# One x turn for four head pairs, one turn for k and q, and a new table of orders and homes

## The chip, the core and the metric

The kernel runs on one core of a Trainium2 chip. Its engines are PE (TensorE, the matrix engine), DVE (VectorE), ACT (ScalarE), POOL (GpSimd) and SP (SyncE, which here only issues transfers). Each engine works through its own list of instructions in order, and waits at an instruction until what it needs is there. The metric is the device time of one execution in microseconds (us), as the median of several runs.

## The reference

Sparse attention, and a maxout layer behind it. Of the attention there are 4 batches, 8 heads, 768 positions and 64 columns a head:

```python
k_sum = k.reshape(B, H, nb, block, D).max(axis=3)       # 24 blocks of 32 keys
v_sum = v.reshape(B, H, nb, block, D).mean(axis=3)
scores_l = scale * q @ k^T, kept where |i - j| < 16
scores_s = scale * q @ k_sum^T + log(32)
a = softmax over both together
attn = a @ concat(v, v_sum)
x = attn.transpose(0, 2, 1, 3).reshape(3072, 512)
g = maximum(x @ w1, x @ w2)                             # 512 -> 1024
out = g @ w_out                                         # 1024 -> 512, float32
```

## The kernel before

**Maxout.** The kernel uses max(h1, h2) = h1 + relu(h2 - h1). It makes wd = w2 - w1 (four tiles of 256 columns) and w1o = w1 · w_out once, and then out = x·w1o + relu(x·wd)·wo. Matmuls are in bf16. On PE, L829 is x·wd (128x256 each), L856 is x·w1o, L863 is g·wo (both up to 128x512), and L813 makes w1o.

**Attention.** Heads go in pairs (4 pairs a batch), queries in groups of 256 (3 groups a batch). For a pair k and q are loaded in float32 (`land`), cast to bf16 (`kqb`), turned so that the head's columns lie on partitions, and k is placed with its block maxima in `kx` (L565 copies, the maxima are L619). Scores (L661) of two pairs and one group fill two banks of PSUM; exp on ACT gives `pb` (L675), DVE masks it (L685), values (L717) multiply with `vx`, and DVE divides by the sum, which gives one half `xs` of the group's x (L741: 128x512, two pairs). x must be turned as well, into `xt`, ahead of L829.

**Turns.** In the first batch, and for k and q of some pairs later, PE turns (L593, L756) and an engine copies the result out of PSUM. For the other three batches x is turned by a DMA transpose that SP issues (L747, 128x4x128: four blocks of 128x128 for one half, so two transfers a group). For the head pairs of `CFG["turn"]` = 22 23 30 31 32 33 (batch, pair) k and q are turned by DMA as well (L597, 128x6x128: one transfer for k, one for q, into `kt`).

**What sets the order.** Each step is a task in one list. A list scheduler (`Plan.run`) goes through time, and gives each free engine the ready task with the lowest number in `CFG["prios"]`; `CFG["engines"]` has a letter per task, its home (P POOL, D DVE, A ACT, S SP, T PE). Tiles come from rings: a task that needs a new tile waits until one of the ring is free. So the two tables and the sizes of the rings decide the order on all five engines, and it is fixed at build time. SP issues all loads, all turns by DMA and nearly all stores, in one order: an issue stands behind those ahead of it. Besides what its data needs, each issue waits for the landing of the transfer issued eight before it.

In the program's order PE ends its turns of batch 0 and w1 first, with fillers (L303) where it would idle; then comes the first L813, once w_out is cast (`wo`, L565); from there on maxout groups and attention of later batches alternate until the last stores.

## Time and profile before

| | |
|---|---|
| median of 3 runs | 170.51 us (169.4, 170.51, 171.54) |
| profiled execution | 169.97 us |
| its span (first to last instruction) | 168.2 us, so 1.77 lies around it |
| PE busy | 159.7 us (95%) |
| DVE, ACT, POOL busy | 104.0, 104.5, 43.1 us |
| moved by DMA | 36.68 MB, mean 218 GB/s |
| turns by DMA | 18 of x, 12 of k or q |

The page's rows of tenths cut the span into 40 equal slices; a digit is the busy share of a slice (9 is 90% or more). A row of a group of instructions has line, engine, operation, out<-in with partitions x elements, count, busy us and mean ns, and the idle time of the engine just ahead of them with what ended it. The chain of waits follows back from the last instruction to whatever released it at each step: start, duration, engine or transfer. SPq is a transfer's issue on SP.

### The profile page before, as it was taken

How to read it: one execution, taken by the hardware profiler on the slowest of the kernel's cores; microseconds unless marked ns; L12 is line 12 of the kernel's file. 1: busy time of each engine (PE TensorE's matmuls, PEld its weight loads, DVE VectorE, ACT ScalarE, POOL GpSimd, SP SyncE). 2: the span in 40 equal slices, each digit the busy share in tenths (PEclk: the TensorE clock that was granted, in tenths of full speed). 3: DMA queues.
4: the chain of work that ended last, by engine and by line, in shares of the span. 5: the costliest groups of instructions: out<-in, count | busy, mean ns of one | idle time of the engine just before them, and what ended most of it. 6: DMA issues, size and time to landing. Idle time of an engine off the chain costs nothing.

```text
span 168.2 us, 4640 instructions
## 1 busy us (share of the span) xinstructions
PE 159.7 (95%) x1918; PEld 105.6 (63%) x1918; DVE 104.0 (62%) x207; ACT 104.5 (62%) x148; POOL 43.1 (26%) x73
## 2 busy tenths in 40 slices
PE   6999999989999999999999999979997999999992
PEld 4768757765676555667577555737564558568462
DVE  4778688663397898787695573849913867023031
ACT  4576888783697998887993578953365652024111
POOL 7506575056534000356330203330300000000000
PEclk9999999999999999999999999999999999999999
DMA  5999999999999999999888998989889336211033
GB/s 166 337 227 329 283 348 351 375 376 313 302 281 320 304 277 233 290 179 216 173 190 241 293 170 212 248 116 238 163 251 162 94 66 181 41 62 64 4 125 125
DMA packets 69829, 36.68 MB, mean 218 GB/s; under 512 B 54640, under 2 KB 65776, under 8 KB 69808
## 3 DMA queue, kind: packets, MB, share of 16 engines
q1 hardware_dynamic: 69664, 36.32, 86.1%
q8 instruction: 15, 0.25, 0.7%
q10 hardware_dynamic: 144, 0.07, 0.1%
q14 instruction: 6, 0.05, 0.1%
HBM read 25.17 MB, written 6.29 MB: 187 GB/s over the span
## 4 chain that ended last, share of the span: by engine, by line
PE 70%; DMA 14%; SPq 9%; POOL 3%; issue 1%; DVE 0%; ACT 0%
PE banks L863 24%; PE banks L829 20%; PE banks L856 11%; DMA land<-in_moe_w_out_dram 6%; DMA land<-in_v_dram 4%; PE banks L813 4%; SPq L463 4%; PE banks L717 4%; PE banks L661 3%; DMA kt<-kqb 3%; SPq L454 3%; PE banks L593 2%; DMA xt<-xs 1%; SPq L597 1%; PE banks L537 1%; POOL vx L565 1%
## 5 line engine op out<-in xcount | busy, mean ns | idle before, releaser
L829 PE MATMUL banks<-xt,wd 128*128 128x256 bf16 x384 | 46.2, 273 | 1.5 <-DMA xt<-xs 1.2
L863 PE MATMUL banks<-wo,g 128*128 128x512 bf16 (+2 forms) x208 | 46.8, 363 | 0.0
L829 PEld LDWEIGHTS <-wd 128*128 128x128 bf16 x384 | 37.2, 98 | 10.3 <-issue 1.5
L863 PEld LDWEIGHTS <-g 128*128 128x128 bf16 x208 | 19.0, 98 | 17.1
L675 ACT ACTIVATE pb<-banks 128x1024 bf16<-128x1024 f32 x24 | 23.8, 1021 | 8.1 <-PE banks L661 8.0
L838 ACT ACTIVATE g<-banks 128x512 bf16<-128x512 f32 x27 | 16.0, 596 | 20.1 <-PE banks L829 19.9
L856 PE MATMUL banks<-w1o,xt 128*128 128x512 bf16 (+2 forms) x104 | 24.6, 363 | 0.0
L840 DVE TENSOR_SCALAR g<-banks 128x512 bf16<-128x512 f32 x21 | 14.3, 687 | 10.1 <-PE banks L829 10.0
L619 DVE TENSOR_REDUCE ks<-kx 128x24 bf16<-128x768 bf16 x16 | 15.1, 949 | 5.7 <-ACT kx L565 5.3
L565 ACT COPY o<-banks 128x512 f32<-128x512 f32 (+1 forms) x16 | 9.1, 575 | 15.3 <-PE banks L863 13.2
L685 DVE TENSOR_TENSOR pb<-pb,mask 128x1024 bf16<-128x1024 bf16 (+1 forms) x24 | 12.6, 557 | 7.8 <-ACT pb L675 7.7
L565 ACT CAST kqb<-land 128x768 bf16<-128x768 f32 x14 | 13.9, 995 | 3.9 <-DMA land<-in_q_dram 1.9
L741 DVE TENSOR_TENSOR xs<-banks,inv 128x512 bf16<-128x512 f32 x24 | 15.9, 678 | 0.3
L565 DVE COPY o<-banks 128x512 f32<-128x512 f32 (+1 forms) x10 | 6.0, 608 | 13.9 <-PE banks L863 13.9
L856 PEld LDWEIGHTS <-xt 128*128 128x128 bf16 x104 | 9.3, 98 | 8.3 <-DMA xt<-xs 0.2
L565 POOL COPY vx<-vx 32x128 bf16<-32x128 bf16 (+5 forms) x10 | 7.6, 769 | 21.7 <-DVE vx L491 12.5
L303 PE MATMUL banks<-ident,identity 128*128 128x256 bf16 x70 | 10.9, 308 | 1.6 <-DVE identity L354 1.6
L661 PEld LDWEIGHTS <-kx 64*128 64x128 bf16 x416 | 7.0, 94 | 7.5 <-issue 7.4
L717 PEld LDWEIGHTS <-pb 128*64 128x64 bf16 (+1 forms) x384 | 8.9, 110 | 4.0 <-issue 1.9
L717 PE MATMUL banks<-vx,pb 128*64 128x65 bf16 (+1 forms) x384 | 11.0, 196 | 0.0
L593 PE MATMUL banks<-ident,kqb 128*128 128x128 f32 x60 | 10.0, 282 | 0.3 <-ACT kqb L565 0.2
L565 DVE CAST kqb<-land 128x768 bf16<-128x768 f32 x12 | 8.2, 693 | 3.3 <-DMA kt<-kqb 1.9
(84 smaller groups left out, 183.9 us busy)
## 6 DMA issues: line engine op xcount, KB each, us to landing
land<-in_k_dram SPq DMA_DIRECT2D x16, 384.0 KB, 6.2
land<-in_q_dram SPq DMA_DIRECT2D x16, 384.0 KB, 5.9
land<-in_v_dram SPq DMA_DIRECT2D x16, 384.0 KB, 6.3
out_dram<-o SPq DMA_DIRECT2D x19, 256.0 KB, 3.9
land<-in_moe_w_dram SPq DMA_DIRECT2D x8, 512.0 KB, 8.2
land<-in_moe_w_out_dram SPq DMA_DIRECT2D x4, 512.0 KB, 9.7
out_dram<-o SPq DMA_DIRECT2D x4, 224.0 KB, 4.3
xt<-xs SPq DMA_TRANSPOSE x18, 2.6
```

The costliest lines, as they stand in the source:

```text
L565: {"D": nc.vector.tensor_copy, "A": nc.scalar.copy, "P": nc.gpsimd.tensor_copy}[e](out=o, in_=i)
L593: nc.tensor.transpose(out=bank(ps)[:, 128 * j:128 * j + 128], in_=src.ap[:].bitcast(F32)[:, 128 * j:128 * j + 128], identity=ident32[:])
L619: op("D", 0.95, lambda e: nc.vector.tensor_reduce(out=ks.ap[:, 0:nb], in_=free(kt(), 128, [256, NM], [192, 2], [32, 2], [1, 32]), axis=AX. ...
L675: op("A", {"A": 1.03}, lambda e: nc.scalar.activation(out=spread(pb.ap[:, 0, 0:1], [192, 8], [128, 2], [1, 64]) if PW > 128 else spread(pb ...
L685: nc.vector.tensor_tensor(out=o, in0=o, in1=spread(mask[:, 2 * u:2 * u + 1, 0:1], [0, n], [64, 2], [1, 64]), op=ALU.mult)
L717: nc.tensor.matmul(out=o, lhsT=p[r], rhs=vx[b].ap[r, par, hp + n, 2 * grp + u, a, 0:D + 1], start=(PW == 128 or par == 0), stop=(last and ...
L741: op("D", 0.69, lambda e: nc.vector.tensor_tensor(out=x.ap[:].rearrange("p n u a d -> p n (u a) d"), in0=spread(bank_tile[:, ps.ap, 0:1], ...
L829: nc.tensor.matmul(out=bank(ps)[:, 256 * s:256 * s + 256], lhsT=wd[n].ap[:, c, 128 * s:128 * s + 128], rhs=x.ap[:, c, :], start=(c == 0), ...
L838: nc.scalar.activation(out=o, in_=bank(ps), func=ACT.Relu)
L840: nc.vector.tensor_scalar_max(out=o, in0=bank(ps), scalar1=0.0)
L856: nc.tensor.matmul(out=bank(ps, c1 - c0), lhsT=x.ap[:, c, sl], rhs=w1o[c].ap[:, cols], start=(c == 0), stop=False)
L863: nc.tensor.matmul(out=bank(ps, c1 - c0), lhsT=g.ap[:, f, sl], rhs=wo[f // 2].ap[:, f % 2, cols], start=False, stop=(f == FC - 1))
```

## The change

Three edits to tiles and transfers, and a new pair of tables.

- x of a group is written into one tile of all four head pairs (`xs`, 128x1024, a ring of three instead of four halves) and turned by one transfer of eight blocks, issued with the second half. The first batch keeps its halves turned by PE.
- k and q of a head pair turned by DMA are cast into the two halves of one tile (`kqm`, a ring of two) and turned by one transfer of twelve blocks into a double `kt` tile (a ring of four).
- To fit, the rings `kqb` (pairs turned by PE) and `o` (outputs) have three tiles instead of four.
- Both tables are replaced in full: the order of all engines changes, and the home of many casts, copies and relus.

```diff
@@ -28,40 +28,40 @@
 CFG["prios"] = list(map(int, """
-36 42 59 141 97 66 223 24 166 102 61 5 160 80 103 211 41 43 38 67 83 12 32 33 49 203 16 170 18 63 98 19 7 118 153
...
+21 237 67 7 280 2 17 63 36 37 59 48 6 33 112 10 49 238 1 23 52 15 120 114 107 9 191 53 14 16 31 102 92 61 24 367 295
...
 """.split()))
 CFG["engines"] = "".join("""
-PDDDPPADDDPPPPPPDPSSSDDDATDASSSDDPPTAASSSPPDPTAASSSPDPPTDDSSDPTASSPDTASSPATDSSDATASPSPSASPDTDTADPDADDTATADPPADATATDD
...
+DPDDPDDPDDPDPPPPPPSSSAPAATADSSSAPDPTDDSSSAAAPTDDSSSDPPDTDDSSPPTASSDPTASSDATDSSDATASASDSASPDTDTDDDDADPTATADPDPDPTPTDD
...
 """.split())
@@ -316,7 +316,8 @@
         return spread(t[:, at:at + 1], *dims)
 
     land = Ring(tiles("land", 13, [128, 1024], F32))
-    kqb = Ring(tiles("kqb", 4, [128, J * 2 * D], BF16))
+    kqb = Ring(tiles("kqb", 3, [128, J * 2 * D], BF16))
+    kqm = Ring(tiles("kqm", 2, [128, 2, J * 2 * D], BF16))
     kxr = Ring(tiles("kx", 4, [128, KW], BF16))
     qxr = Ring(tiles("qx", 6, [128, S], BF16))
     PW = 128 if CFG["cols"] else 192
@@ -325,11 +326,11 @@
     stg = Ring(tiles("sums", 2, [128, H // 2, VW], BF16))
     apart = tiles("apart", 2, [128, H, VW], BF16)
     ksr = Ring(tiles("ks", 3, [128, 32], BF16))
-    ktr = Ring(tiles("kt", 6, [128, J, 128], BF16))
-    xsr = Ring(tiles("xs", 4, [128, 2, 2, 2, D], BF16))
+    ktr = Ring(tiles("kt", 4, [128, 2, J, 128], BF16))
+    xsr = Ring(tiles("xs", 3, [128, NP, 2, 2, D], BF16))
     xtr = Ring(tiles("xt", 6, [128, KC, GT], BF16))
     gr = Ring(tiles("g", 3, [128, FC, GT], BF16))
-    osr = Ring(tiles("o", 4, [128, d_model], F32))
+    osr = Ring(tiles("o", 3, [128, d_model], F32))
     wd = [Buf(Ring([t])) for t in tiles("wd", 4, [128, KC, 256], BF16)]
     w1br = Ring(tiles("w1b", 2, [128, KC, 256], BF16))
     w1b = [Buf(w1br) for _ in range(4)]
@@ -572,15 +573,15 @@
     def prep(b, hp, prio, k_on, q_on, kp, qp, tail_on):
         kx[b, hp] = Buf(kxr)
         tag = f"{b}{hp}"
-        pss = []
+        pss, by_dma = [], f"{b}{hp}" in CFG["turn"]
+        both = Buf(kqm), Buf(ktr)
         for n, eng in enumerate((k_on, q_on)):
-            by_dma = f"{b}{hp}" in CFG["turn"]
-            f, src, ps = kqin[b, hp, n], Buf(kqb), Buf(ktr) if by_dma else Buf(banks, "kq")
+            f, src, ps = kqin[b, hp, n], both[0] if by_dma else Buf(kqb), both[1] if by_dma else Buf(banks, "kq")
             pss.append(ps)
 
             def cast(f=f, src=src, n=n):
                 if by_dma:
-                    return (src.ap[:].rearrange("p (j h d) -> p h j d", h=2, d=D),
+                    return (src.ap[:, n].rearrange("p (j h d) -> p h j d", h=2, d=D),
                             landed(f, 2, J * D).rearrange("p h (j d) -> p h j d", d=D))
                 return (src.ap[:].rearrange("p (i h d j) -> p h i j d", h=2, d=D, j=2),
                         landed(f, 2, J * D).rearrange("p h (i j d) -> p h i j d", d=D, j=2))
@@ -594,15 +595,17 @@
                                         in_=src.ap[:].bitcast(F32)[:, 128 * j:128 * j + 128], identity=ident32[:])
 
             if by_dma:
-                op("S", 0.65, lambda e, src=src, ps=ps: nc.sync.dma_start_transpose(out=ps.ap[:], in_=src.ap[:]),
-                   read=[src], write=[ps], prio=prio, issue=1.35, words=60, label=f"turn {'kq'[n]}{tag}")
+                if n:
+                    op("S", 1.3, lambda e, src=src, ps=ps: nc.sync.dma_start_transpose(
+                        out=ps.ap[:].rearrange("p n j t -> p (n j) t"), in_=src.ap[:].rearrange("p n c -> p (n c)")),
+                       read=[src], write=[ps], prio=prio, issue=1.7, words=60, label=f"turn kq{tag}")
             else:
                 op("T", J * 0.056, lambda e, turn=turn: turn(), words=J, read=[src], write=[ps], prio=prio, label=f"turn {'kq'[n]}{tag}")
 
         kps, qps = pss
 
         def order(ps, *dims):
-            return spread(ps.ap[:].rearrange("p j t -> p (j t)") if by_dma else bank(ps, S, BF16), *dims)
+            return spread(ps.ap[:, 0].rearrange("p j t -> p (j t)") if by_dma else bank(ps, S, BF16), *dims)
 
         def kt():
 
@@ -643,7 +646,7 @@
 
         def q_of(n, r, c0, c1):
             t = qx[b, hp + n].ap
-            return (t if len(t.shape) == 2 else t[:].rearrange("p j t -> p (j t)"))[r, c0:c1]
+            return (t if len(t.shape) == 2 else t[:, 1].rearrange("p j t -> p (j t)"))[r, c0:c1]
 
         def mm():
             if mask_on == "T":
@@ -731,23 +734,27 @@
             op("T", 0.26 if b else 0.51, lambda e, n=n: mm(n), words=16 if b else 32, read=[pb, ready[b, hp + n], *([] if b else [apart_of[hp + n]])],
                touch=[vx[b]], write=[ps], prio=prio, label=f"values {tag}{n}")
         inv = Buf(invr)
-        x = Buf(xsr)
+        whole = xt_on == "S"
         if hp == 0:
             xt[b, grp] = Buf(xtr)
-        x_t = xt[b, grp]
+        if hp == 0 or not whole:
+            xs[b, grp] = Buf(xsr)
+        x, x_t = xs[b, grp], xt[b, grp]
+        at_x = hp if whole else 0
         op("D", 0.21, lambda e: nc.vector.reciprocal(
             out=inv.ap[:], in_=spread(bank_tile[:, ps.ap, D:D + 1], [512, 2], [D + 1, 4])),
            read=[ps], write=[inv], prio=prio, label=f"inv {tag}")
         op("D", 0.69, lambda e: nc.vector.tensor_tensor(
-            out=x.ap[:].rearrange("p n u a d -> p n (u a) d"),
+            out=x.ap[:, at_x:at_x + 2].rearrange("p n u a d -> p n (u a) d"),
             in0=spread(bank_tile[:, ps.ap, 0:1], [512, 2], [D + 1, 4], [1, D]),
             in1=spread(inv.ap[:, 0:1, 0:1], [4, 2], [1, 4], [0, D]), op=ALU.mult),
            read=[ps, inv], write=[x], prio=prio, label=f"x {tag}")
-        if xt_on == "S":
-            op("S", 0.45, lambda e: nc.sync.dma_start_transpose(
-                out=x_t.ap[:, hp:hp + 2, :].rearrange("p h (u n) -> p (h u) n", u=2),
-                in_=x.ap[:].rearrange("p h u a d -> p (h u a d)")),
-               read=[x], write=[x_t], prio=prio, issue=1.3, words=60, label=f"xt {tag}")
+        if whole:
+            if hp:
+                op("S", 0.85, lambda e: nc.sync.dma_start_transpose(
+                    out=x_t.ap[:].rearrange("p h (u n) -> p (h u) n", u=2),
+                    in_=x.ap[:].rearrange("p h u a d -> p (h u a d)")),
+                   read=[x], write=[x_t], prio=prio, issue=1.4, words=60, label=f"xt {tag}")
             return
         xp = Buf(banks, "x")
 
```

SP's list goes from 122 to 107 rows, PE's fillers from 70 to 77; the number of other matmuls stays. Where PE goes from 64-wide attention groups to 512-wide groups there are 21 places instead of 18. Behind the edits lines move: L597 becomes L599, L747 L754, L829 L836, L856 L863, L863 L870, L565 L566, L741 L747, L874 L881.

**SP, late in batch 2: turns for batches 2 and 3 of attention.** `xt` are x turns, `kt` turns of k and q, `land` loads, `out_0` stores. Before:

```order
L747 DMA_TRANSPOSE xt0_113<-xs3_112 128x4x128
L597 DMA_TRANSPOSE kt5_108<-kqb1_76 128x6x128
L747 DMA_TRANSPOSE xt2_115<-xs0_109 128x4x128
L454 DMA land0_62<-in_q_dram 128x12x64
L597 DMA_TRANSPOSE kt0_103<-kqb3_78 128x6x128
L454 DMA land10_72<-in_q_dram 128x12x64
L597 DMA_TRANSPOSE kt1_104<-kqb2_77 128x6x128
L747 DMA_TRANSPOSE xt0_113<-xs2_111 128x4x128
L597 DMA_TRANSPOSE kt2_105<-kqb3_78 128x6x128
L597 DMA_TRANSPOSE kt3_106<-kqb1_76 128x6x128
L597 DMA_TRANSPOSE kt4_107<-kqb2_77 128x6x128
L874 DMA out_0_dram<-o2_124 128x512
```

And now, from the turn of the first of batch 3's head pairs on:

```order
L599 DMA_TRANSPOSE kt2_106<-kqm1_79 128x12x128
L754 DMA_TRANSPOSE xt0_111<-xs2_110 128x8x128
L599 DMA_TRANSPOSE kt3_107<-kqm0_78 128x12x128
L881 DMA out_0_dram<-o2_122 128x512
L881 DMA out_0_dram<-o0_120 112x512
L883 DMA out_0_dram<-o0_120 16x512
L599 DMA_TRANSPOSE kt0_104<-kqm1_79 128x12x128
L754 DMA_TRANSPOSE xt1_112<-xs0_108 128x8x128
L599 DMA_TRANSPOSE kt1_105<-kqm0_78 128x12x128
L881 DMA out_0_dram<-o1_121 128x512
L881 DMA out_0_dram<-o2_122 128x512
L881 DMA out_0_dram<-o0_120 128x512
```

The loads among the turns are gone from here (they stand further ahead), and no three turns of k and q stand in a row any more: a turn of a pair has an x turn or stores between it and the next.

**SP, the start: the last weights.** Before:

```order
L774 DMA land6_68<-in_moe_w1_dram 128x4x256
L454 DMA land7_69<-in_k_dram 128x2x384
L799 DMA land8_70<-in_moe_w_out_dram 128x2x512
L799 DMA land9_71<-in_moe_w_out_dram 128x2x512
L799 DMA land10_72<-in_moe_w_out_dram 128x2x512
L799 DMA land11_73<-in_moe_w_out_dram 128x2x512
L774 DMA land12_74<-in_moe_w2_dram 128x4x256
L454 DMA land1_63<-in_k_dram 128x2x384
```

Now:

```order
L781 DMA land6_68<-in_moe_w1_dram 128x4x256
L806 DMA land7_69<-in_moe_w_out_dram 128x2x512
L455 DMA land8_70<-in_k_dram 128x2x384
L806 DMA land9_71<-in_moe_w_out_dram 128x2x512
L806 DMA land10_72<-in_moe_w_out_dram 128x2x512
L806 DMA land11_73<-in_moe_w_out_dram 128x2x512
L455 DMA land12_74<-in_k_dram 128x2x384
L455 DMA land0_62<-in_k_dram 128x2x384
L455 DMA land1_63<-in_k_dram 128x2x384
L781 DMA land2_64<-in_moe_w2_dram 128x4x256
```

The first w_out load has changed places with a k load, and the last w2 load stands behind three k loads.

More of the change, by code (lines that the diff above doesn't have):

```diff
@@ L30 @@
 CFG["prios"] = list(map(int, """
[25 rows of a table removed]
[25 rows of a table added]
 """.split()))
 CFG["engines"] = "".join("""
[L58 to L64 removed]
+DPDDPDDPDDPDPPPPPPSSSAPAATADSSSAPDPTDDSSSAAAPTDDSSSDPPDTDDSSPPTASSDPTASSDATDSSDATASASDSASPDTDTDDDDADPTATADPDPDPTPTDD
+DPAAATDTDDPPPATATDDTDTATDDTATATDDTDTATDDTDTATDDTDTATDDTDSSSASSSPSSSDSSSADPDPPPPPTDDDDDDTATDDPDPAPTDTADDPADTADTDDTADT
+DDTADTDDDTPTADDDDDDTATADAAADTADTDDSTADTDDSTADTDDSSSSDSSSDSSSPSSSADPAADPDSTAAPADATATDDPPADATATADADDDTADTDDTADTDDTADTD
+DAASADPPPAPSADPPPTADTDDSTADTDDSTADTDDSSSSASSSASSSASSSAPDDPPDPPTAAAPAPDSADPPAADSDDDPPTADTDDTADTDDTADTDDADSADPDAPPSDDD
+PATADTDDSTADTDDSTADTDDSTTATTATTATTDTDTDTATATTTDSTTTDSTATATDTDTTTDSTTTASTATATATATTTASTTTDSTDTDTATDTTTASTTTDSTDTATATDT
+TTASTTTASTATDTDTATTTDSTTTASTATDTDTDTTTDSTTTASTATDTATATTTASTTTASTATDTDTDTTTASTTTDSTATATATATTTASTTTASTDTATDTATTTDSTTTA
+STATDTATDTTTASTTTASTTTDATTTDS
 """.split())
```

6 lines of the change are left out of this document (removed), and 48 rows, old and new, of the table turn.

## The prediction

> **What bounds the kernel now.** I read the page first, for the busiest engine, its clock and the DMA engines.
>
> ```profile
> span 168.2 us, 4640 instructions
> ...
> PE 159.7 (95%) x1918; PEld 105.6 (63%) x1918; DVE 104.0 (62%) x207; ACT 104.5 (62%) x148; POOL 43.1 (26%) x73
> ...
> PEclk9999999999999999999999999999999999999999
> DMA  5999999999999999999888998989889336211033
> ```
>
> TensorE works 95% of the span at full granted clock; the DMA engines are full for its first three quarters. Then stretches (each row: PE busy, PEld, DVE, ACT, POOL, granted clock, DMA share, GB/s).
>
> ```profile
> 37.30:165.00 127.70, 125.51 (x1382) 79.78 (x1381) 76.83 (x147) 77.47 (x108) 25.00 (x33) 1.00 0.83 194
> 0.00:37.30 37.30, 34.01 (x537) 25.81 (x537) 26.66 (x59) 26.99 (x41) 18.11 (x40) 1.00 1.04 309
> 165.00:168.20 3.20, 0.20 (x4) 0.03 (x1) 0.52 (x2) 0.00 (x0) 0.00 (x0) 1.00 0.37 123
> ```
>
> There are three stages. Up to 37.30 the program waits for bytes (DMA share 1.04). From there to 165.00 PE is busy 125.51 of 127.70 and idle 2.19. The last 3.20 are copies and stores. PE's waits name the idle time:
>
> ```profile
> PE banks L829 <- DMA xt<-xs: 1.2, 1, 1.2
> PE banks L661 <- DMA kt<-kqb: 1.0, 1, 1.0
> PE banks L813 <- POOL wo L565: 0.8, 1, 0.8
> ```
>
> The first two are the whole 2.19 of the middle stage; the third ends the start. The chain of waits (start, duration, what) shows how they came about.
>
> ```profile
> 26.75 9.40 DMA land<-in_moe_w_out_dram
> 36.21 1.05 POOL wo L565
> 37.30 2.75 PE banks L813 x12
> ...
> 105.65 0.97 PE banks L856 x4
> ...
> 108.58 2.32 SPq L597
> 111.00 2.49 DMA xt<-xs
> 113.53 1.91 PE banks L829 x16
> ...
> 118.91 0.86 PE banks L856 x4
> ...
> 124.01 5.13 DMA kt<-kqb
> 129.28 0.41 PE banks L661 x16
> ...
> 151.28 4.37 PE banks L829 x40
> ```
>
> The start ends with a w_out load landing at 36.2 and its cast. At 113.5 PE waits for an x turn that stood on SP behind a k/q turn holding SP for 2.32. At 129.3 it waits for a k/q turn that took 5.13 to land. So at most 2.19 can be had from the change in the middle stage; anything else must come from the start or the tail.
>
> **The change, part by part.** The sum runs against the profiled execution: 169.97, span 168.2 and 1.77 around it; the median of the runs is 0.54 higher.
>
> *Work on PE: +0.2 to +0.3.* Matmuls are the same in number, save seven fillers (L303) more, all in the start. The new order goes from the 64-wide attention groups to 512-wide ones 21 times instead of 18. In the chain four L856 take 0.97 where attention stands ahead of them (105.65) and 0.86 elsewhere (118.91), so three more switches cost about 0.3 at most. Middle work becomes 125.5 + 0.2 = 125.7.
>
> *The start: +0.15.* PE waits for the second w_out load to be issued (wo0). The k load and the first w_out load ahead of it have only changed places, so it lands at 36.2 again. Its cast moves from POOL to ACT.
>
> ```profile
> 36.21 1.04 POOL L565 CAST wo<-land 128x1024 bf16<-128x1024 f32 x1 [0.23 <-DMA land<-in_moe_w_out_dram]
> 38.93 1.05 ACT L565 CAST wo<-land 128x1024 bf16<-128x1024 f32 x1 [1.27 <-DMA land<-in_moe_w_out_dram]
> 40.45 2.35 POOL L777 TENSOR_TENSOR wd<-land,land 128x1024 bf16<-128x1024 f32 x1 [1.63 <-DMA land<-in_moe_w_dram]
> 31.16 1.22 DVE L777 TENSOR_TENSOR wd<-land,land 128x1024 bf16<-128x1024 f32 x1 [1.35 <-DMA land<-in_moe_w_dram]
> ```
>
> ACT's cast takes 1.05, POOL's 1.04: w1·wo starts at 37.45. The PE work ahead of it ends by 36.95 by my count, so half a microsecond covers it. The last w2 load goes behind three k loads: it landed at 40.4 (POOL's subtraction began there) and now lands near 43.6. POOL's 2.35 becomes DVE's 1.22, behind a relu already in DVE's queue: wd2 is ready at about 45.7, and PE first reads it at about 46.1. Nothing is lost, with 0.4 in hand; a load 1 us later costs 0.6.
>
> *Turns, their price.* No row has an 8- or 12-block turn. Of the present ones (issue min/median/max ns; landing us):
>
> ```profile
> L747 SPq DMA_TRANSPOSE xt<-xs x18: 1195/1216/2818, 68.5 to 142.6; - x18
> ...
> DMA to landing us min/median/max: 2.4/2.6/4.7
> ```
>
> ```profile
> L597 SPq DMA_TRANSPOSE kt<-kqb x12: 1222/1368/3827, 73.9 to 124.0; - x12
> ...
> DMA to landing us min/median/max: 2.7/2.8/4.7
> ```
>
> Four blocks of 128x128 (128 KB) hold SP 1.22, six (192 KB) 1.37: 0.075 a block, so about 1.5 for eight and 1.8 for twelve. For landing I look at two x turns nearly alone (40 slices of 0.15 us, from 140 on):
>
> ```profile
> DMA  8999998993000000499996100599960000000000
> GB/s 300 451 355 369 369 396 328 382 369 82 14 0 14 27 27 27 90 230 232 225 137 33 17 5 0 102 215 215 213 125 4 0 0 0 0 0 0 0 0 0
> ```
>
> The last hump is one turn: about 215 GB/s for 0.6 us, out of a landing of 2.6. The rest is fixed. Twice the bytes add 0.6 to an x turn (3.2) and 0.9 to a k/q turn (3.7). From below: as today, 2.6 and 2.8. From above: two of today's in series, 5.2 and 5.6. I take 3.2 and 3.7 and keep both ends.
>
> The Trainium skill, "DMA: Bandwidth & Descriptors", section "Anatomy of one DMA", fits a transfer as some 2.0 us fixed plus its bytes at 436 GB/s; by it the new turns would be estimated at 2.6 and 2.9. The trace agrees on the fixed part and not on the rate (215), so I don't use it; the sum would be the same by either.
>
> *Turns, what they are late for.* I lay PE's groups of the new order end to end from 37.45, 0.109 for each L829 (40 in 4.37) and 0.216 for a 512-wide one (4 in 0.86). Behind the first read of the last x tile (xt5 of batch 3) stand 56 of the first and 70 of the second kind: 6.1 + 15.1 = 21.2. PE ends near 164.0, so the tile is wanted at 142.8. Its last half leaves DVE at about 138.0, and its turn goes out behind xt4's, at 138.3: landed at 141.5. **Slack 1.3.** The same count for the others (wanted, landed):
>
> - batch 1 x tiles: 74.2 / 72.1, 86.0 / 82.1, 91.7 / 89.4;
> - batch 2 x tiles: 106.9 / 103.7, 110.4 / 108.3, 116.5 / 114.9;
> - batch 3 xt3 and xt4: 137.1 / 134.6, 141.9 / 140.0;
> - batch 3 keys: turns issue at about 102.9, 106.0, 109.6 and 112.6 (before, the last four stood between 115 and 125.5). The last needs two casts on POOL that start once the turn of 106.0 has landed (109.7) and given its kqm tile back; it lands at 116.3, is copied on DVE from 119.4 on (behind an o copy that waits for PE) and its kx is ready at 123.5; PE wants it at 124.5. So landing has 3.1 to spare before DVE, and DVE's chain 1.0.
>
> So both present waits, 2.19, go: the k/q turns come about 10 us earlier, and no x turn has three k/q turns ahead of it. What is late next is xt4 and xt5 of the last batch and kx's chain on DVE.
>
> *Halves that wait.* An x turn now waits for the second half; the first half gets no head start of its own. The wanted/landed list has this in it already (the second half decides). Each half is one row of 0.68:
>
> ```profile
> L741 DVE TENSOR_TENSOR xs<-banks,inv 128x512 bf16<-128x512 f32 x24 | 15.9, 678 | 0.3
> ```
>
> *Shorter rings.* Three o tiles instead of four: a copy waits for the store three tiles back, and relus and casts on DVE and ACT stand behind it.
>
> ```profile
> out_dram<-o SPq DMA_DIRECT2D x19, 256.0 KB, 3.9
> ```
>
> At 3.9 the tightest, the o2 copy on DVE at 107.9, has its store (issued near 101.9) landed at 105.8: 2.1 in hand. At the end stores meet quiet queues; two copies there stand about 1 us clear. I cost it at 0; a store slower by 3 us costs 1 each time.
>
> *Small waits.* A dozen places stand within 0.4 of late (wd2; the vx cast near 72; a mask near 82.5). From below they cost nothing; at a third of them 0.3 each is 1.2. I take 0.9.
>
> **Sum.** 37.45 + 125.7 + 0.9 + 3.2 = 167.2 of span, 1.0 below 168.2. Own time 169.0; on the median's scale **169.5**.
>
> **Rivals.**
>
> - *B, the gain is eaten.* The start slips (wd2 1 us later: +0.6) and the small waits reach 1.2: span 168.1, time 170.4. For it: the start is DMA-bound at share 1.04, and a changed load order reaches PE at once there. Against: the bytes ahead of wo0 are the same.
> - *C, slower: the turns are pulled into full DMA engines.* Of stretches of ten:
>
> ```profile
> 50.00:60.00 10.00, 10.00 (x128) 6.27 (x126) 8.07 (x17) 8.77 (x14) 2.15 (x5) 1.00 1.15 308
> 60.00:70.00 10.00, 10.00 (x152) 5.18 (x151) 8.63 (x20) 8.90 (x14) 1.64 (x2) 1.00 1.18 266
> ...
> 100.00:110.00 10.00, 10.00 (x112) 6.25 (x109) 6.01 (x11) 8.87 (x12) 2.77 (x2) 1.00 1.04 216
> ...
> 130.00:165.00 35.00, 35.00 (x360) 22.99 (x356) 13.63 (x26) 11.21 (x17) 0.00 (x0) 1.00 0.29 80
> ```
>
> All loads and all k/q turns are now to be done by 116 instead of 129, with the same bytes, while 100 to 110 is at share 1.04 already. Loads in the crowd land in about 6:
>
> ```profile
> land<-in_v_dram SPq DMA_DIRECT2D x16, 384.0 KB, 6.3
> ```
>
> Were the turns to land in 6.3, x tiles (3.1 later) would miss by 1.0, 1.0 and 1.5 in batches 1 and 2 and by 1.8 in batch 3, 1.8 in all, since a wait shifts what comes after it. The last keys would come 2 x 2.6 = 5.2 late with 4.1 to spare: 1.1, to be added if the turns themselves shift with PE. Sum +2.9: span 170.1, time 172.4. It decides from landings of about 4.5 for x (smallest slack 1.3) and of 5.7 for k/q. For it: the 5.13 in the chain. Against: the medians of 2.6 and 2.8 were taken in this same crowd. At 7.5 it would be 174 and more.
> - *D, little comes together.* The first wait goes and a like one comes, at xt4 or at kx: one of the two, +1.1, time 170.6; counted with B.
> - *E, no wait at all and a start as before.* 37.3 + 125.7 + 3.2 = 166.2, time 168.5. More would need an earlier start, and wo0's load keeps its place.
>
> **How the numbers follow.** Forecast 0.45 (168.8 to 170.2), B with D 0.22 (170.2 to 171.5), C 0.27 (171 to 175, most near 172.4), E 0.06. A change within 2% (167.1 to 173.9) is about what a measurement of this kernel can't tell from none. Faster by more needs a span under 164.8, 1.4 below E: 0.03. Slower by more is the upper third of C: 0.1. The range leaves out half of E and the upper end of C: 168.2 to 173.2.
>
> **What would show it.** The 1.2 and 1.0 of the two DMA waits gone; the w1·wo start at 37.3 to 37.6; x turns landing near 3.2 and k/q turns near 3.7; PE busy 125.6 to 125.9 from there on; idle in the middle under 1.2; the tail at 3.2. I am wrong if the turns land in over 4.5, if PE waits for kx or xt in batch 3, if a copy of o waits for its store, or if the start moves by over 0.5.

## The result, and the profile after

The changed kernel takes **170.62 us** (median of 20 runs, 169.93 to 171.97), the kernel before 169.44 (20 runs, 167.99 to 171.54): a ratio of **1.0095, 95% interval 1.007 to 1.0119**. It is slower by about 1%, where I had forecast 0.6% faster. By the bound of 2% it is no change; by its interval it is slower. Ratios below leave out executions more than 1.5% above the fastest of the same kernel; where a kernel spreads so widely that this matters, the median of all its runs stands beside the ratio.

The profiled execution of the changed kernel (169.93) is its fastest of 20, and that of the kernel before (169.97) lies above its median, so these two pages look alike though the kernels are not. I read the page first (busy time, granted clock, DMA share in tenths), and then three stretches cut at the first w1·wo matmul and at PE's end (PE, PEld, DVE, ACT, POOL busy, clock, DMA share, GB/s).

```profile
span 168.1 us, 4611 instructions
...
PE 157.8 (94%) x1903; PEld 106.4 (63%) x1925; DVE 105.6 (63%) x208; ACT 104.1 (62%) x137; POOL 48.0 (29%) x83
...
PEclk9999999999999999999999999999999999999999
DMA  5999999999999998999999999999400739000314
```

```profile
36.97:164.80 127.83, 124.39 (x1364) 79.46 (x1385) 77.37 (x145) 79.61 (x106) 28.29 (x40) 1.00 0.83 190
0.00:36.97 36.97, 33.45 (x539) 26.97 (x540) 27.87 (x62) 24.46 (x32) 19.71 (x43) 1.00 1.06 315
164.80:168.10 3.30, 0.00 (x0) 0.00 (x0) 0.33 (x2) 0.00 (x0) 0.00 (x0) 0.90 0.50 167
```

The DMA engines are now full without a break until about 118 us, and then nearly idle for ten. The middle stretch is 127.83 long; in the kernel before, from 37.30 to the end of its last matmul at 165.21, it was 127.91. (Some 21 matmuls are missing from the records of this stretch, 1364 beside 1385 weight loads, so its busy time reads too low; I go by lengths.) PE's waits:

```profile
PE banks L863 <- DMA xt<-xs: 0.8, 1, 0.8
PE banks L820 <- ACT wo L566: 0.5, 1, 0.5
PE banks L863 <- ACT o L566: 0.4, 1, 0.4
```

Both waits of the kernel before are gone: L836 waits for no x turn at 113, and L664 for no k/q turn at 129. In their place stand 0.8 for another x turn and 0.4 for an o copy. The chain of waits shows where the 0.8 is from:

```profile
26.42 9.38 DMA land<-in_moe_w_out_dram
35.88 1.05 ACT wo L566
...
104.45 5.38 DMA kt<-kqm
...
110.60 1.52 ACT kx L566
...
112.62 1.23 SPq L599
...
113.90 3.83 DMA xt<-xs
...
117.78 1.04 PE banks L863 x4
```

A k/q turn lands after 5.38; ACT and then SP stand behind it; SP issues the next k/q turn at 112.2 (the chain counts it from 112.62, when ACT is done with the copy and the relu behind it) and only then, at 113.9, the last x turn of batch 2, which lands 3.83 later. It is the same pattern as in the kernel before, one tile further on.

One profiled execution of each is too few here, so the kernels were profiled again, unaltered. "Start" is the start of the first w1·wo matmul, "middle" from there to the end of PE's last matmul, "tail" the rest of the span:

| kernel | start | middle | tail |
|---|---|---|---|
| before | 37.30, 36.51, 37.03, 36.40: mean 36.81 | 127.91, 127.93, 127.80, 128.32: mean 127.99 | 2.99, 2.96, 2.97, 2.98: mean 2.98 |
| changed | 36.97, 38.08, 37.74, 36.84, 38.77: mean 37.68 | 127.83, 128.07, 127.89, 127.84, 127.46: mean 127.82 | 3.30, 3.45, 3.37, 3.42, 3.37: mean 3.38 |
| difference | +0.87 | -0.17 | +0.40 |

The sum is +1.10, beside the 1.18 between the medians. So the middle, where the gain was to be, gave 0.17; start and tail, which I had left nearly as they were, took 1.27.

PE's waits in the middle can be added up by execution. All those of 0.15 and more make 2.19, 1.92, 1.60 and 1.81 in the kernel before (mean 1.9) and 1.21, 1.73, 1.49, 1.47 and 1.04 in the changed one (mean 1.4). So 0.5 of waits went, and PE's time without them grew by the other 0.3. The page on which the forecast rested shows the largest waits of the four: its x turn and its k/q turn, 2.19 together, make 1.54, 1.16 and 1.32 in the other three.

### The profile page after: what moved, and what is told of

It is laid out like the page before. It is cut to its first block, busy times and chain, and to the rows that moved or that the text cites. A ratio compares the mean times of both kernels' runs of the same rounds, so it can differ in the third digit from the quotient of the medians.

```text
span 168.1 us, 4611 instructions
## 1 busy us (share of the span) xinstructions
PE 157.8 (94%) x1903; PEld 106.4 (63%) x1925; DVE 105.6 (63%) x208; ACT 104.1 (62%) x137; POOL 48.0 (29%) x83
## 4 chain that ended last, share of the span: by engine, by line
PE 75%; DMA 13%; ACT 4%; issue 2%; DVE 1%; SPq 1%; POOL 1%; POOLq 0%; ACTq 0%
PE banks L870 19%; PE banks L836 17%; PE banks L863 12%; PE banks L303 6%; DMA land<-in_moe_w_out_dram 6%; PE banks L594 4%; PE banks L820 4%; PE banks L664 4%; PE banks L720 3%; DMA kt<-kqm 3%; DMA xt<-xs 2%; DMA out_dram<-o 2%; PE banks L538 1%; PE banks L655 1%; ACT pb L678 1%
## 5 line engine op out<-in xcount | busy, mean ns | idle before, releaser
L836 PE MATMUL banks<-xt,wd 128*128 128x256 bf16 x384 | 46.9, 273 | 0.1
L870 PE MATMUL banks<-wo,g 128*128 128x512 bf16 (+2 forms) x196 | 44.2, 362 | 1.4 <-issue 1.3
L836 PEld LDWEIGHTS <-wd 128*128 128x128 bf16 x384 | 37.0, 98 | 9.0 <-DMA xt<-xs 0.6
L870 PEld LDWEIGHTS <-g 128*128 128x128 bf16 x208 | 18.5, 98 | 17.1 <-issue 0.2
L845 ACT ACTIVATE g<-banks 128x512 bf16<-128x512 f32 x26 | 15.4, 598 | 21.6 <-PE banks L836 21.6
L863 PE MATMUL banks<-w1o,xt 128*128 128x512 bf16 (+2 forms) x96 | 23.9, 361 | 1.6 <-DMA xt<-xs 0.8
L566 POOL COPY vx<-vx 64x1584 bf16<-64x1584 bf16 (+5 forms) x16 | 14.0, 884 | 20.5 <-DVE vx L492 9.4
L566 DVE COPY o<-banks 128x512 f32<-128x512 f32 (+1 forms) x11 | 6.7, 616 | 20.0 <-PE banks L870 18.6
L688 DVE TENSOR_TENSOR pb<-pb,mask 128x1024 bf16<-128x1024 bf16 (+1 forms) x24 | 13.6, 596 | 6.1 <-ACT pb L678 6.0
L566 ACT COPY o<-banks 128x512 f32<-128x512 f32 (+1 forms) x15 | 8.6, 571 | 13.7 <-PE banks L870 11.1
L747 DVE TENSOR_TENSOR xs<-banks,inv 128x512 bf16<-128x512 f32 x24 | 15.9, 680 | 0.4
L863 PEld LDWEIGHTS <-xt 128*128 128x128 bf16 x104 | 9.7, 98 | 10.0 <-DMA xt<-xs 1.3
L303 PE MATMUL banks<-ident,identity 128*128 128x256 bf16 x77 | 12.1, 310 | 2.2 <-DVE apart L395 2.2
L720 PEld LDWEIGHTS <-pb 128*64 128x64 bf16 (+1 forms) x384 | 8.9, 110 | 5.6 <-issue 4.0
L566 POOL COPY kx<-kx 128x384 bf16<-128x384 bf16 (+1 forms) x17 | 6.4, 380 | 19.9 <-DVE kx L566 11.8
L720 PE MATMUL banks<-vx,pb 128*64 128x65 bf16 (+1 forms) x384 | 10.8, 196 | 0.8 <-issue 0.8
L303 PEld LDWEIGHTS <-identity 128*128 128x128 bf16 x77 | 8.4, 111 | 3.9 <-DVE apart L395 2.2
L664 PEld LDWEIGHTS <-kx 64*128 64x128 bf16 x416 | 7.0, 94 | 6.0 <-issue 5.9
```

The source lines that it names most:

```text
L303: nc.tensor.matmul(out=bank_tile[:, slot, 0:256], lhsT=identity[:], rhs=ident32[:].bitcast(BF16), start=True, stop=True)
L566: {"D": nc.vector.tensor_copy, "A": nc.scalar.copy, "P": nc.gpsimd.tensor_copy}[e](out=o, in_=i)
L720: nc.tensor.matmul(out=o, lhsT=p[r], rhs=vx[b].ap[r, par, hp + n, 2 * grp + u, a, 0:D + 1], start=(PW == 128 or par == 0), stop=(last and ...
L747: op("D", 0.69, lambda e: nc.vector.tensor_tensor(out=x.ap[:, at_x:at_x + 2].rearrange("p n u a d -> p n (u a) d"), in0=spread(bank_tile[: ...
L836: nc.tensor.matmul(out=bank(ps)[:, 256 * s:256 * s + 256], lhsT=wd[n].ap[:, c, 128 * s:128 * s + 128], rhs=x.ap[:, c, :], start=(c == 0), ...
L845: nc.scalar.activation(out=o, in_=bank(ps), func=ACT.Relu)
```

## The experiments

### Half of the late loads' bytes left out

Two theories at first. *Full DMA engines*: the turns were pulled into a stretch in which the engines have no room, so they land late and SP and the o copies stand behind them. *Order*: the new order has chains of its own that DMA has no part in. The edit, in both kernels, for k, q and v of batches 2 and 3:

```diff
-    out=landed(f, 2, J * D), in_=src[b, 2 * hp:2 * hp + 2].rearrange("h (p j) d -> p h (j d)", j=J))
+    out=landed(f, 2, J * D)[:, :, 0:J * D // (2 if b > 1 else 1)],
+    in_=src[b, 2 * hp:2 * hp + 2].rearrange("h (p j) d -> p h (j d)", j=J)[:, :, 0:J * D // (2 if b > 1 else 1)])
```

(and likewise one of the two heads where q and v are loaded with positions on partitions; what is left out keeps an earlier load's values).

> The changed kernel with half of the bytes of every k, q and v load of batches 2 and 3 left out (the other half of the tile keeps what an earlier load put there); order, homes, turns and all else stay. Theory 'full DMA engines' (the turns were pulled into a stretch where the DMA engines have no room, so they land in 4.0 to 5.4 us instead of 3.2 and 3.7, and SP and the o copies stand behind them): turns land in 3.0 to 3.4 (x) and 3.3 to 3.8 (k and q), PE's waits for xt (0.8) and for an o copy (0.4) go, and the time falls by 1 to 2 us, to a ratio of 0.997 to 1.003 to the kernel before. Theory 'order' (the new order has chains of its own between PE, DVE and ACT that DMA has no part in): the ratio stays at 1.007 to 1.012.

> The kernel before with the same half of the bytes left out. Theory 'full DMA engines': the kernel before has room for its turns already and gains less than the changed one, 0.3 to 1 us (its idle times at the xt and kt waits shrink): ratio 0.994 to 0.998. If it gains as much as the changed kernel or more, the crowd is no peculiarity of the change, and the 0.95% must have another cause.

Measured: the changed kernel 0.9981 (0.9946 to 1.0017), the kernel before 0.9884 (0.9848 to 0.992). Both gain, 1.1% (from 1.0095) and 1.2% of the kernel before. So the crowd costs both kernels about alike, and it isn't what parts them: with room on the DMA engines the changed kernel is still 1% behind. The middle stretch of the one and the other:

```profile
38.37:164.38 126.01, 123.92 (x1364) 79.50 (x1385) 77.53 (x145) 79.30 (x106) 28.89 (x40) 1.00 0.67 155
```

```profile
36.96:162.44 125.48, 123.53 (x1359) 79.76 (x1381) 78.52 (x149) 77.79 (x109) 25.34 (x33) 1.00 0.68 161
```

With DMA share at 0.67 neither waits for a turn, and the floor of the middle shows: 126.0 with the new tables, 125.5 with the old. So the full DMA engines cost the kernel before 127.99 - 125.48 = 2.5 in the middle, and the changed one 127.82 - 126.01 = 1.8. By these two executions, one of each kernel, the change saves 0.7 of what the crowd costs, and its order takes 0.5 of that back; the waits added up above give 0.5 and 0.3. The rest of the difference between these two runs is the start (38.37 against 36.96) and the tail (3.4 against 2.9).

The turns still landed in 4.3 (x) and 4.1 (k/q) in the light run of the changed kernel, by their medians, and not in 3.0 to 3.4 and 3.3 to 3.8 as expected. So the waits did not go because turns land sooner; they went because SP issues them sooner. The last x turn of batch 2 in the light run, and unaltered:

```profile
113.08 1.64 SPq L755 DMA_TRANSPOSE xt<-xs  x1
```

```profile
113.90 1.72 SPq L754 DMA_TRANSPOSE xt<-xs  x1
```

Counted from the first w1·wo matmul these are 74.7 and 76.9 (76.6 to 77.1 in all five unaltered executions). The turn lands after 3.7 in the one and 3.7 to 3.8 in the others, so PE's wait is decided by the issue. Of the 2.2, 1.6 arise at the x turn two before it: it holds SP for 1.3 in the light run and for 2.91 in the unaltered one.

### One part of the change at a time

The turns split again in place, each into two of half the size behind one another, with the changed kernel's order:

```diff
-    nc.sync.dma_start_transpose(out=x_t.ap[:]..., in_=x.ap[:]...)
+    [nc.sync.dma_start_transpose(out=x_t.ap[:, h:h + 2]..., in_=x.ap[:, h:h + 2]...) for h in (0, 2)]
```

> The changed kernel with each turn split again in place: an x turn into two of 128x4x128, a k/q turn into two of 128x6x128, one behind the other on SP, order and rings as in the changed kernel. Theory 'merging costs' (one long turn lands later than two short ones, and holds SP as long): ratio falls to 1.002 to 1.006. Theory 'full DMA engines': the bytes and the place decide, not the number; SP has nine x and six k/q issues of 1.2 to 1.4 more to make, some 20 us in all, so equal or slower, 1.009 to 1.02.

Measured: 1.0634 (1.0591 to 1.0678), far above the expectation's upper end. The x turns and their landing (issue min/median/max ns), and PE's waits:

```profile
L754 SPq DMA_TRANSPOSE xt<-xs x18: 1200/1258/4077, 70.7 to 151.0; - x18
...
DMA to landing us min/median/max: 2.4/2.6/6.4
```

```profile
PE banks L836 <- DMA xt<-xs: 2.8, 3, 1.7
...
PE banks L863 <- ACT o L566: 1.4, 1, 1.4
...
PE banks L863 <- DMA xt<-xs: 1.4, 2, 0.7
```

A half turn lands in 2.6 again, but fifteen more issues of 1.26 are 19 us of SP's time, and everything that SP issues comes later. So in this order SP's queue is what counts, and merging is worth up to 5% to it; "merging costs" falls. A part of the 5% is TensorE's clock: right behind PE's waits of 1.65 and 0.92 at 117 and 118, the granted clock was 0.50 for 3.41 us (last three columns clock, DMA share, GB/s).

```profile
117.99:121.40 3.41, 3.16 (x15) 2.16 (x15) 1.63 (x3) 1.90 (x3) 0.01 (x1) 0.50 0.78 183
```

At half the clock that is an estimated 1.7 us, 1% of the kernel. No profile of the kernel before or of the changed one has such a stretch in its middle.

The other half of the change was taken alone: merged turns and new rings, with the tables of the kernel before (the entries of the 15 turns that are gone left out).

> The merged turns and the changed rings with the tables of the kernel before (the entries of the 15 turns that are gone left out): one part of the change alone. Theory 'merging is free or helps, the new tables cost': 0.995 to 1.005. Theory 'merging costs where the order was not made for it' (a half of x waits for the other, an o ring of three): 1.01 to 1.03.

Measured: 1.0333 (1.0247 to 1.0419), and the middle is 135.07. PE's waits:

```profile
PE banks L835 <- ACT g L844: 1.9, 1, 1.9
...
PE banks L835 <- DMA xt<-xs: 1.3, 2, 1.1
PE banks L835 <- DVE g L846: 1.1, 2, 0.6
PE banks L593 <- DVE o L565: 0.9, 1, 0.9
```

Of these waits 1.3 are for x turns themselves. The largest, 1.9, is for a relu on ACT, and ahead of it ACT stood 2.81 for a k/q turn (its cast at 113.71). So an order made for halves waits for wholes; how much of the loss belongs to the ring of three o tiles (0.9 is for an o copy) was not parted from this. Here too the granted clock was 0.50 for 3.41 us, from 76.94 on, behind waits of 0.85 and 1.09: 1.7 us of the 5.3 by the same estimate. The one start of this kernel is that of the old tables, 36.46, so nothing says that the new tiles and their places in memory delay the start. The converse, new tables with the old turns and rings, has no run.

### The ring of o

Four o tiles, the fourth on a `w1b` tile that is dead by then, with the order unchanged. In the first version the tiles are taken strictly in turn, so that one can be written again ahead of its store, and a part of the output is another tile's; the second takes a free one and never has more than three in use.

```diff
-    osr = Ring(tiles("o", 3, [128, d_model], F32))
+    osr = Ring(tiles("o", 3, [128, d_model], F32) + [None], {"o": 3})
...
+    osr.slots[3] = w1br.slots[0][:].rearrange("p c n -> p (c n)").bitcast(F32)
```

> The changed kernel with its order unchanged, but the o tiles taken in turn from four (the fourth lies on a w1b tile that is dead by then). Theory 'shorter ring of o': the wait of the ACT copy for a store at 85 us (2.0 us, 0.4 of it on PE) goes, and so do like ones in other executions: 0.4 to 1.2 us less, ratio 1.002 to 1.007. Theories 'full DMA engines' and 'order': within 0.2% of the changed kernel, 1.008 to 1.011, since the late stores are only one of the things that stand behind SP.

> The changed kernel with four o tiles again, now with a free one taken each time (never more than three in use, so the order stays), where the earlier one took them strictly in turn and could give a tile away before its store. Theory 'shorter ring of o': 1.002 to 1.007. Theories 'full DMA engines', 'start' and 'order': 1.007 to 1.012, as without it.

Measured: 1.0116 (1.0064 to 1.0169) and 1.0048 (1.0007 to 1.0089). The second lies within the band of the theory "shorter ring", but its interval meets that of the unaltered kernel on another chip (1.0065, 1.0026 to 1.0104, below), and its profiled middle is no shorter (129.46). The wait for an o copy is gone from its trace; x turns at 113 and relus at 92 wait more instead. At best 0.2 to 0.5% hang on the ring; for the whole time this is not settled.

For the tail it is clearer. With the fourth tile taken when free, the tail is 3.0 to 3.1 in both profiles (this one and the one with three mends below), beside 3.30 to 3.45 in the changed kernel. The last two whole o copies on ACT with three tiles (PE ends at 164.80), and the first of the two with four (166.83):

```profile
162.95 1.17 ACT L566 COPY o<-banks 128x512 f32<-128x512 f32 x2 [4.05 <-PE banks L870]
```

```profile
164.66 0.58 ACT L567 COPY o<-banks 128x512 f32<-128x512 f32 x1 [3.73 <-PE banks L871]
```

The first of the two begins 1.85 ahead of PE's end with three tiles and 2.17 with four. So 0.3 of the 0.4 in the tail go with the ring of three, in an order that is otherwise the same.

### The start

The second profiles were taken to see whether the first ones were usual.

> The kernel before once more, for a second profiled execution. Theory 'little to gain' (the profiled execution of before, 169.97, was slower than its median of 169.44 and its two waits of 2.19 were larger than usual): from the first w1·wo matmul to PE's last one 126.5 to 127.5 instead of 127.9, waits for xt and kt 0.3 to 1.5 in sum. If it is 127.9 again with 2.19 of waits, the waits belong to the order and the change did remove them.

> The changed kernel once more. Its profiled execution (169.93) was the fastest of its 20 runs, so a usual one is 0.7 longer: theory 'full DMA engines' puts that into the middle (waits for xt, kt and o copies 1.5 to 2.5 instead of 1.2); theory 'start' puts it ahead of the first w1·wo matmul (37.5 to 38.5 instead of 36.97, as in the two kernels of the first group whose loads began late).

> The changed kernel unaltered, timed on the same chip as the next three, as their yardstick: 1.007 to 1.012. Its profile is one more sample: first w1·wo matmul at 37.0 to 38.4, then 127.8 to 128.2 to PE's end, tail 3.2 to 3.5.

> The kernel before, for one more profiled start. Theory 'the start belongs to the tables': first w1·wo matmul at 36.4 to 37.3 as in the four executions with its tables so far, w loads begin at 15.4 to 16.7. Theory 'chance': also 37.4 to 38.7 occurs, as with the new tables.

> The changed kernel, for one more start on the same chip. 'The start belongs to the tables': first w1·wo matmul mostly at 37.4 or later. 'Chance': 36.5 to 37.3 as often as later.

> The kernel before, one more start: 'the start belongs to the tables' has it at 36.4 to 37.3 again, 'chance' at up to 38.7.

> The changed kernel, one more start: 'the start belongs to the tables' has it mostly at 37.4 or later, 'chance' at 36.5 to 37.3 as often.

Measured: the table above. "Little to gain" holds in one half: the kernel before has both waits in all four executions (1.21, 0.84, 0.24 and 0.25 for the x turn, 0.98, 0.70, 0.92 and 1.07 for the k/q turn), but the 2.19 of the first was the largest sum. Its other half falls: the middle is 127.8 to 128.3 each time, and not 126.5 to 127.5. The unaltered changed kernel as control gave 1.0065 (1.0026 to 1.0104), single runs 171.33, 169.83 and 171.38. "Start" stands: with the old tables, including three kernels edited only later in the program (36.96, 36.46, 36.34), all seven starts lie at 36.3 to 37.3; with the new ones, including five kernels edited only later (38.37, 36.81, 38.70, 37.38, 37.43), seven of ten lie above 37.3. Three more are of kernels below: 37.39 and 39.56 with the new tables and an early load exchanged, and 38.41 with the old tables, in an execution that took 172.16. With them it is nine late starts of twelve beside one of eight. The latest of the changed kernel and an early one of the kernel before:

```profile
38.77 1.89 PE L820 MATMUL banks<-wo,w1t 128*128 128x512 bf16 x7 [1.15 <-ACT wo L566]
```

```profile
36.51 2.75 PE L813 MATMUL banks<-wo,w1t 128*128 128x512 bf16 x11 [0.40 <-POOL wo L565]
```

Both wait for the cast of the w_out load. The first 16 us of these two executions (last two columns DMA share and GB/s):

```profile
0.00:16.00 16.00, 13.78 (x149) 10.65 (x150) 10.88 (x29) 7.91 (x9) 10.30 (x32) 1.00 0.96 251
```

```profile
0.00:16.00 16.00, 14.35 (x145) 10.45 (x146) 10.96 (x28) 10.15 (x15) 7.17 (x28) 1.00 0.99 266
```

A part of the late start is there by 16 us: 15 GB/s less over 16 us are 0.24 MB, or 0.8 us at the 315 GB/s that the changed kernel moved up to w_out. But the w_out load lands 2.24 later (37.60 beside 35.36). From 16 us to these landings:

```profile
16.00:37.60 21.60, 19.83 (x392) 15.57 (x391) 15.96 (x33) 15.62 (x22) 9.39 (x12) 1.00 1.06 343
```

```profile
16.00:35.36 19.36, 18.82 (x386) 15.21 (x384) 14.68 (x30) 15.76 (x25) 9.86 (x11) 1.00 1.08 341
```

The rate is the same there, but the engines move 7.41 MB before the load has landed, and 6.60 in the other: the 0.24 that was behind and another 0.57, though the same number of loads and bytes is issued ahead of it. Which transfers these are isn't shown.

The four executions of the kernel before moved 262 to 266 GB/s in the first 16 us, those of the changed one 267 and 264 (starts 36.97, 36.84) or 246 to 252 (37.74, 38.08, 38.77). In all twelve profiles with the new tables 259 to 267 goes with starts up to 36.97, and 243 to 252 with starts from 37.38 on. The start of 38.41 with the old tables has 264, so a start can also be late without it. The one difference in kind among the first ten loads is that a load of v stands ahead of one of k. That was put back:

```diff
+        for a, b in [("load k02", "load v01")]:
+            (move a ahead of b in the order)
```

> The changed kernel with one pair of issues exchanged in the first ten on SP: the load of k of pair 2 goes ahead of the first v load again, as in the kernel before; all else stays. Theory 'start by load order' (the early v load is why the first w1·wo matmul comes at 36.8 to 38.7 instead of 36.5 to 37.3): it comes at 36.5 to 37.3 and the ratio is 0.3 to 0.5% under the control's. Theory 'start by chance' (the spread of the start has nothing to do with this pair): start and ratio as the control's.

Measured: 1.0081 (1.0043 to 1.0118), as the control; and the kernel with three mends, which has this exchange too, starts at 37.39. So nothing speaks for this pair. That the start of the new tables is often late is shown, and that a low rate of the first loads goes with it; **why the rate falls, and why more is moved before w_out lands, stays open**.

### An x turn behind a k/q turn

The last x turn of batch 2 goes ahead of the k/q turn in front of it.

```diff
+        for a, b in [("xt 221", "turn kq31")]:
+            (move a ahead of b in the order)
```

> The changed kernel with one pair of issues exchanged late on SP: the last x turn of batch 2 (wanted near 117) goes ahead of the k/q turn that stands in front of it. Theory 'a new wait of the old kind' (an x turn behind a k/q turn on SP, as in the kernel before): PE's wait of 0.8 at that x tile goes, the k/q turn comes 1.0 to 1.6 later within its slack, and 0.4 to 0.8 us are saved, 0.25 to 0.5% under the control. Rival: the k/q turn becomes late in its place and PE waits for its keys at 120 to 125 instead, no gain.

> The changed kernel with three mends together: four o tiles (a free one each time), the k load ahead of the v load, the x turn ahead of the k/q turn. If the mends add up (0.45% for o by the earlier run, 0.3 to 0.5% and 0.25 to 0.5%): 0.995 to 1.001. If what is left is the order's own (its floor of 126.0 against 125.5 in the runs with fewer bytes, a tail 0.3 longer): not under 1.000.

Measured: 1.0037 (0.9996 to 1.0079), and with o and the loads mended too 1.0041 (0.9998 to 1.0085), control 1.0065. In the trace the mechanism is as expected: no wait for an x turn is left at 118. What stands there instead (PE, and then DVE):

```profile
88.97 1.02 PE L867 MATMUL banks<-w1o,xt 128*128 128x512 bf16 x4 [0.87 <-ACT o L570]
...
121.44 1.03 PE L840 MATMUL banks<-xt,wd 128*128 128x256 bf16 x8 [0.54 <-DVE o L570]
```

```profile
118.89 0.83 DVE L570 COPY kx<-kt 128x768 bf16<-128x768 bf16 x1 [1.69 <-DMA kt<-kqm]
119.75 0.18 DVE L570 COPY kx<-kx 128x32 bf16<-128x32 bf16 x1
119.84 0.95 DVE L626 TENSOR_REDUCE ks<-kx 128x24 bf16<-128x768 bf16 x1
120.70 0.68 DVE L570 COPY o<-banks 128x512 f32<-128x512 f32 x1
```

The k/q turn that went behind lands at 118.87 (116.37 in the changed kernel); DVE waits 1.69 for it, the o copy stands behind in DVE's queue, and PE waits for the o copy. That is the rival of the expectation in another place: the k/q turn is late, and PE pays at the o copy and not at the keys. The middle is 128.41. The gain of 0.3% is inside the interval. The mends don't add up: three together are no better than one.

### The same two waits, mended in the kernel before

If the two waits were only a matter of SP's order, they could be had without merged turns. The last q turn of batch 3 goes ahead of three stores; in the other kernel an x half also goes ahead of a k turn.

```diff
+        for a, b in [("turn q30", "store 200"), ("xt 202", "turn k30")]:
+            (move a ahead of b in the order)
```

> The kernel before (old turns, rings and tables) with two pairs of issues exchanged on SP: the last x half of group 202 goes ahead of the k turn that stands in front of it (its x is ready at 106.6, the k turn holds SP from 108.6 to 110.9), and the last q turn of batch 3 goes ahead of three stores. Theory 'the two waits are SP's order alone': both PE waits (0.2 to 1.2 at 113, 0.7 to 1.1 at 129) go and nothing takes their place, 1.0 to 1.9 us less: ratio 0.988 to 0.994, ahead of both kernels. Theory 'full DMA engines': the landing is what is late, a place on SP alone gains little: 0.996 to 1.000.

> The kernel before with the second exchange alone (the last q turn ahead of the three stores). Theory 'SP's order alone': the wait of 0.7 to 1.1 at 129 goes: 0.994 to 0.997. Theory 'full DMA engines': 0.998 to 1.001, since the three k turns ahead of it still fill the engines.

Measured: with both 0.9921 (0.9857 to 0.9985), but this rests on the 4 fastest of 12 runs; the median of all twelve is 171.07, with runs from 167.6 to 176.1, beside 170.05. With the one alone 0.9984 (0.9928 to 1.0039); median of all 171.88. Neither can be called faster. The trace of the second shows why (PE, and then ACT):

```profile
128.57 0.41 PE L665 MATMUL banks<-kt,kx 64*128 64x64 bf16 x16 [1.88 <-ACT pb L679]
129.48 0.45 PE L721 MATMUL banks<-vx,pb 128*64 128x65 bf16 x16 [0.51 <-ACT pb L679]
```

```profile
127.00 0.58 ACT L569 COPY o<-banks 128x512 f32<-128x512 f32 x1 [3.87 <-DMA out_dram<-o]
127.49 1.95 ACT L679 ACTIVATE pb<-banks 128x1024 bf16<-128x1024 f32 x2
```

The keys are there in time now. But the three stores come later, an o copy on ACT waits 3.87 for one of them, the exp stands behind this copy in ACT's queue, and PE waits 1.88 + 0.51 for the exp: more than the 0.7 to 1.1 that was taken away.

## Why the prediction was wrong

**"Both present waits, 2.19, go": right, but 2.19 was too much to count on.** The two waits make 2.19, 1.54, 1.16 and 1.32 in the four executions of the kernel before, 1.55 on average. The k/q turn is waited for in none of the five executions of the changed kernel, the x turn near 113 in one (0.43 at 111.5). The steps behind it held too: no wait at wd2, none at xt4 and xt5 of the last batch, kx in time, clock full.

**"Small waits: I take 0.9": this step failed.** Cut at PE's end, as in the table above, the forecast middle was 126.8, 0.2 more than when cut at 165.00: 125.9 of work and 0.9 of waits. It came to 127.8. The work was about right: the light run, where PE waits for nothing, has 126.0. Above it stand 1.8 and not 0.9; of these PE's own waits are 1.4 on average, and the trace doesn't name the rest. The largest is for the x tile "116.5 / 114.9", which landed at 117.7; PE waited for it in all five executions, 0.68 to 0.85. By its own landing of 3.2 I had its turn issued at 111.7. It went out at 113.90 and landed 3.83 later: 2.2 too late by the issue and 0.6 by the landing. The k/q turns of batch 3 show the same: they went out at 104.45, 108.70, 112.23 and 115.73, where I had 102.9, 106.0, 109.6 and 112.6. That the issue decides is shown by the light run, where the turn lands no sooner and PE doesn't wait.

The landings were taken too low as well, at 3.2 and 3.7. Min/median/max for x and for k/q:

```profile
DMA to landing us min/median/max: 3.3/4.0/6.4
```

```profile
DMA to landing us min/median/max: 3.7/4.2/6.0
```

In the other four executions the medians are 4.5 to 4.6 and 4.3 to 4.6. My step from 128 KB to 256 KB added only the time that the last 128 KB moved; the shortest landing is near it, the usual one isn't. Of the last three x turns, when little else runs, the one alone takes 3.3 and two issued 1.3 apart take 4.1 and 3.7. Rival C had the turns land in 6.3; what came late is SP's issue, at a place that I had named, and it cost 0.7 to 0.85 there and not 1.5.

What the issue of a turn costs SP was estimated too high, at 1.5 and 1.8: the shortest of eight blocks took 1.24 and of twelve 1.27, hardly more than 1.20 and 1.22 for four and six. SP's time goes by the number of issues.

The Trainium skill, "DMA: Bandwidth & Descriptors", section "Anatomy of one DMA", would by its fit, which is for transfers issued by GpSimd, have put these landings at an estimated 2.6 and 2.9. The shortest in the trace are 3.3 and 3.7, so by that fit the landings would have been forecast further off.

**"The start: +0.15": this step failed.** It rested on equal bytes ahead of the w_out load and on its landing at 36.2. The bytes issued ahead are equal, the landing isn't: in three of five executions the first loads run at 246 to 252 GB/s, the latest one also moves more before w_out has landed, and the start is 0.87 later on average. Why stays open. My base was off as well: 37.30 is the latest of the four starts of the kernel before. Rival B had a later start, but by wd2, which never waited.

**"Tail: 3.2 again": this step failed too, by 0.4**, and is the plainest of all. The last stores of the kernel before and of the changed one (those issued after 164 us; KB, us to landing):

```profile
out_dram<-o SPq DMA_DIRECT2D x1, 256.0 KB, 2.1
out_dram<-o SPq DMA_DIRECT2D x1, 64.0 KB, 1.6
out_dram<-o ACTq DMA_DIRECT2D x1, 64.0 KB, 1.6
```

```profile
out_dram<-o SPq DMA_DIRECT2D x1, 256.0 KB, 2.3
out_dram<-o SPq DMA_DIRECT2D x1, 64.0 KB, 2.1
out_dram<-o ACTq DMA_DIRECT2D x1, 64.0 KB, 2.0
out_dram<-o SPq DMA_DIRECT2D x1, 32.0 KB, 2.1
```

In the new order two whole o tiles are copied and stored in the last 2 us where it was one and a half, so the last 64 KB land 0.4 to 0.5 later. I had looked at whether those copies would wait for their tiles, found them 1 us clear and put the shorter rings at 0, and had not looked at what lies in the queue beside the last store. With four o tiles the copies begin 0.3 earlier and the tail is 3.0 to 3.1, so 0.3 of the 0.4 belongs to the ring of three.

**In sum:** of the forecast changes, that of the middle was 0.9 too low (-1.1 beside -0.17), that of the start 0.7 and that of the tail 0.4, together about the 2.1 between -1.0 and +1.1. The time stayed in the range, its direction was wrong. That the forecast of 169.5 is only 1.1 off is in part luck: it stood on a median of three runs, 170.51, and twenty runs give 169.44 for the kernel before.

## What to carry to other kernels

A wait that comes from one full queue seldom goes by itself when the queue's order is changed: here each exchange on SP took one wait away and made another of like size, because stores, turns and loads share SP and the DMA engines, and copies stand in order behind what waits for a store or a turn. When an order is replaced in full, price the first load's landing and the last store's as carefully as the middle, and take the base from several profiled executions: two pages of equal length hid a difference of 1%. Fewer, larger transfers pay by the issues they save, but a merged transfer lands later than its half did, and its consumers need that slack. A tile taken from a ring can show its price in the tail alone.

## What was not expected

- The issue of a DMA turn hardly depends on its size: at least 1.20, 1.22, 1.24 and 1.27 us for 4, 6, 8 and 12 blocks of 128x128. Its landing does: shortest 2.4, 2.7, 3.3 and 3.7, medians 2.6, 2.8, 4.0 and 4.2.
- With the new tables PE stands still for 0.5 to 1.5 us near 26 us in the middle of a values group (L720 of the changed kernel), for nothing that the profile shows; that is so in all twelve executions with them and in none of the eight with the old ones. The wait for w_out comes after it, so it didn't set the start. In all twelve PE goes on 1.3 to 1.7 us after the second transfer of the DMA queue "q8 instruction" (16 KB) has ended; that it waits for program code is a guess that no run tests.
- Leaving out half the bytes of the k, q and v loads of two batches in four made the two kernels 1.1 and 1.2% faster, though TensorE is 94 to 95% busy in both.
